# Turned weight blocks routed through device memory, and the value products moved within their step

## The chip, the cores and the metric

The kernel runs on one NeuronCore of one Trainium2 chip. The metric is the device time of that core in microseconds (us), from one execution of the whole program; the median of three runs is compared.

## The reference

Two parts follow one another. The first is an attention with a threshold, for 8 batches of 8 heads, 576 positions and head size 64, in float32:

```python
scores = scale * np.matmul(q, k.transpose(0, 1, 3, 2))          # scale = 1/8
thresh = np.max(scores, axis=-1, keepdims=True) - tau           # tau = 0.02
scores = np.where(scores >= thresh, scores, -1000000000.0)
attn = np.exp(scores - np.max(scores, axis=-1, keepdims=True))
attn = attn / (np.sum(attn, axis=-1, keepdims=True) + 1e-09)
x = np.matmul(attn, v)                                          # heads joined: 4608 tokens x 512
```

The second is an MLP over the 4608 tokens: `h = x @ w_in` (512 to 2048), `g = max(h, 0)**2`, `out = g @ w_out` (2048 to 512).

## The kernel before

**Visits and steps.** The program works on pairs of heads; there are 32 of them (4 per batch). The pairs of the first batch are visited twice, the others once, which makes 36 "visits". A visit has one step for each block of 128 queries (blocks 0 to 3) and one for the last 64 queries (block 4). From visit 12 on, two visits run together ("paired"): the even one begins with block 4 for both, then come blocks 0 to 3 of the even visit and blocks 0 to 3 of the odd one, nine steps in all. There are twelve such double visits, and `late_step` is the loop body for them. The steps before them are built by the body at the end of the file.

**What a step does.** TensorE makes scores into PSUM (`scores_of_two`, L282: on even blocks it makes this step's scores and the next one's). VectorE takes the row maxima (L303), ScalarE the exponents (L318), VectorE compares with the threshold and sums (L330), GpSimd divides (L340). The product with the values needs the weights with the keys on the partitions, so they have to be turned. From visit 11 on this is done in two moves. VectorE transposes 32 x 32 squares into the tile `turned` (`turn_blocks`, L417 to L427). Then DMAs carry squares from one group of 32 partitions to another, into the tile `wT` (`place_blocks`, L437 for blocks 0 to 3, L442 and L450 for block 4). `turned` has two halves of 2304 float32 per partition, used in turn. One half holds a pair of blocks: pair 0 is blocks 0 and 1, pair 1 is blocks 2 and 3, pair 2 is block 4. A block pair 0 or 1 goes over in 16 DMAs: for each of the 4 groups of source partitions (`qb`) and each of the 4 groups of target partitions (`j`) one DMA of 32 partitions x 2304 bytes. All of them are issued on SyncE's queue (SP), which works in order.

**The value product.** `mix` (L486) is 40 matmuls of TensorE that multiply the values by `wT`: the group "one" in PSUM bank 0 reads the columns ONE and LEFT (or ODD and ONE) of `wT`, the group "two" in bank 4 reads the columns TWO, which pair 1 fills. Group one is issued first. `put` copies the result to the tile `xT` on ScalarE (L469, L473, L480). Bank 0 and bank 4 overlap the score areas of even steps. `mixes` says in which step a visit's product stands: for an even visit that is the step of block 3 of the odd visit, for an odd visit the step of block 1 of the next double visit; both are odd steps in which no scores are made. At the last step, END, nothing else is left of the attention.

**What fills the rest.** The MLP is cut into pieces of 8 or 16 matmuls (`piece`, L534, L642, L713, L748), which wait in the deque `waiting`; a chunk of 256 tokens adds its pieces when the value product that completes its tokens has been issued (`add_chunk`). `rate(s)` plans how many us of pieces a step takes, from PIECE_US (1.76), from `other(s)` (what scores and value products take in a step; VALUES_US is 4.8) and from a reserve of three pieces that is to be left when a new chunk comes. `fill(quarter)` issues pieces for a quarter of that. The order of the instructions on each engine is the order in which the program writes them; `after()` and `some_later()` write pending work that follows pieces or prepares them on the other engines.

**In `late_step`** the order was: scores, maxima, exponents, then `values()` (the `mix` of this step if there is one), a quarter of pieces, threshold and divide, a second quarter when the step has no `mix`, `turn_last` (which turns the step before's block and places what `place_at` lists), then the other quarters. `place_at` lists, for a double visit that begins at step s: block 4 at s+1 and s+2, pair 0 and 1 of the even visit at s+3 and s+5, pair 0 and 1 of the odd visit at s+8 and s+9. Their products stand at s+8 and s+11.

Of the kernel before, what the change touches and what calls it, by code (L numbers as in the profile page):

```python
# [9 lines left out]
FP32 = mybir.dt.float32  # L10
# [9 lines left out]
def kernel(  # L20
# [10 lines left out]
    nc = tc.nc  # L31
# [3 lines left out]
    P = 128  # L35
    HP = H // 2
    NPAIR = B * HP
    NBLK = S // P
    REST = S - NBLK * P
# [10 lines left out]
    ctx.enter_context(tc.manual_schedule(engines={getattr(mybir.EngineType, e) for e in MANUAL}))  # L50

    const = ctx.enter_context(tc.tile_pool(name="const", bufs=1))
    psum = ctx.enter_context(tc.tile_pool(name="psum", bufs=1, space=bass.MemoryType.PSUM))

    ident = const.tile([P, P], FP32, name="ident")
# [19 lines left out]
    ODD, ONE, LEFT, TWO = 0, REST, REST + 2 * P, 2 * REST + 2 * P  # L75
    wT = const.tile([P, S // REST + 1, NC9, REST], FP32, name="wT")
# [3 lines left out]
    at = RAW * 2 * WP  # L80
# [12 lines left out]
    NB = 2 * KB * 2 * 32  # L93
    turned = const.tile([P, 2 * NB], FP32, name="turned")
    assert 3 * 3 * WP <= 2 * NB
    g = const.tile([P, NFT, TCH], FP32, name="g")
    gsum = [const.tile([P, HF, P], FP32, name=f"gsum{i}") for i in range(2)]
    held = const.tile([P, 2 * HD], FP32, name="held")
# [97 lines left out]
    def some_loads():  # L196
        for _ in range(min(1 + (len(loads) > 8), len(loads))):
            to, src = loads.popleft()
            (nc.gpsimd if state["step"] > first_dma + 2 else nc.sync).dma_start(out=to, in_=src)
# [193 lines left out]
            nc.scalar.copy(wT[:, 2 * NBLK, NBLK, :], ps[:, 0, 0:D])  # L393

    blocks = {}

    def turn_blocks(vis, i):

        w = weights[vis, i][0]
        two = i < NBLK
        M = KB - 2
        if not two or i % 2 == 0:
            at = len(blocks) % 2 * NB
            t = turned[:, at:at + NB]
            blocks[vis, i // 2] = t.rearrange("p (j c u q) -> p c j u q", j=4, u=2, q=32) if two else t.rearrange("p (k q) -> p k q", q=32)
        wb = blocks[vis, i // 2]  # L410
        move = nc.vector.transpose
        if two:
            wb = wb[:, :, :, i % 2, :]
            whole_, rest_ = (w[:, :, x0 * 32:x1 * 32].rearrange("p u (c j q) -> p u c j q", q=32, j=n)
                             for x0, x1, n in ((0, M, 4), (M, KB, 2)))
            h = M // 4
            move(wb[:, 0:h, :, :], whole_[:, 0, :, :, :])  # L417
            if i < 2:
                move(wb[:, h, :, :].rearrange("p (u j) q -> p u j q", u=2), rest_[:, :, 0, :, :])
            else:  # L420
                move(wb[:, h, 2:4, :], rest_[:, 0, 0, :, :])
                move(wb[:, h, 0:2, :], rest_[:, 1, 0, :, :])
            move(wb[:, h + 1:, :, :], whole_[:, 1, :, :, :])
            return
        parts = [(0, 0, KB, 0), (1, M, KB, KB), (1, 0, M, KB + 2)] if paired(vis) else [(0, 0, KB, 2), (0, M, KB, 0)]
        for u, k0, k1, at in parts:
            move(wb[:, at:at + k1 - k0, :], w[:, u, k0 * 32:k1 * 32].rearrange("p (k q) -> p k q", q=32))  # L427

    def place_blocks(vis, pair, which=range(4)):

        wb = blocks[vis, pair]
        for qb in which:
            rows = slice(qb * 32, qb * 32 + 32)
            for j in range(4):
                to = wT[j * 32:j * 32 + 32, :, :, :]
                if pair < NBLK // 2:
                    nc.sync.dma_start(out=to[:, (ONE, TWO)[pair] // REST + qb, :, :].rearrange("p c q -> p (c q)"),  # L437
                                      in_=wb[rows, :, j, :, :].rearrange("p c u q -> p (c u q)"))
                    continue
                at = slice(qb % 2 * 32, qb % 2 * 32 + 32)  # L440
                if paired(vis):
                    nc.sync.dma_start(out=to[:, (LEFT if qb < 2 else ODD) // REST, :, at], in_=wb[rows, j:2 * KB:4, :])  # L442
                else:


                    first = j if qb < 2 else KB + (j - KB) % 4
                    n = len(range(first, KB if qb < 2 else 2 * KB, 4))
                    c = first // 4
                    first += 2 if qb < 2 else -KB
                    nc.sync.dma_start(out=to[:, LEFT // REST, c:c + n, at], in_=wb[rows, first:first + 4 * n - 3:4, :])  # L450
# [151 lines left out]
    def some_later(engine):  # L602
        if later[engine]:
            make(*later[engine].popleft())
# [201 lines left out]
    steps = [(n, i) for n in range(len(visits)) for i in visits[n][1]]  # L806
    NST = len(steps)

    def by_dma(n):

        return n >= 3 * HP - 1
# [5 lines left out]
    mixes = {}  # L817
# [14 lines left out]
    END = max(mixes)  # L832

    chunk_at, j = {}, 0
# [5 lines left out]
    VALUES_US = 4.8  # L840
    SCORES_US = 1.25
    RESERVE = 3 * PIECE_US
    waiting = deque()
    state = {"us": 0.0, "left": 0.0, "step": 0, "free": False, "rounded": 0, "usable": 0, "then": [], "last": []}

    def early():
        return state["step"] < min(chunk_at)
# [20 lines left out]
    def rate(s):  # L868


        if s < out_from:
            return PIECE_US * sum(x[2] == 0 for x in waiting) / (out_from - s)
        have = PIECE_US * len(waiting) - state["left"]
        best = 1e9
        at = s
        for e in sorted(chunk_at) + [END]:
            if e > s:
                have += sum(other(x) for x in range(at, e))
                at = e
                best = min(best, (have - (RESERVE if e < END else 0)) / (e - s))  # L880
                have += PIECE_US * sum(len(pieces_of(x)) for x in chunk_at.get(e, ()))
        return max(best, 0.0) - other(s)

    def other(s):

        us = VALUES_US if s in mixes and by_dma(mixes[s][0]) else 0.0
        if s < NST:
            n, i = steps[s]
            us += SCORES_US * (1 if s < first_late or i == NBLK else 0 if i % 2 else 2)
        return us  # L890

    def after():
        now = state["last"]
        state["last"] = []
        for fn in state["then"]:
            state["last"] += fn() or []
        state["then"] = []
        for fn in now:
            fn()

    def piece():
        _, fn, *what = waiting.popleft()
        state["left"] -= PIECE_US
        if fn is mlp_out or what[0] <= PLAIN and what[1] == 0:
            after()
        then = fn(*what)
        after()
        state["then"] = then
        if state["step"] >= NST:
            some_later("vector")  # L910
            some_later("gpsimd")

    def fill(us):
        state["left"] += us
        while waiting and state["left"] >= PIECE_US / 2 and waiting[0][0] <= state["usable"]:
            piece()
        state["left"] = min(state["left"], PIECE_US)
# [72 lines left out]
    def turn_last(s):  # L990
        if s <= NST:
            turn_blocks(*steps[s - 1])
        for what in place_at[s]:
            place_blocks(*what)

    def late_step(s):

        on = s < NST
        odd = on and steps[s][1] % 2 == 1
        if on:  # L1000
            n, i = steps[s]
            if not odd:
                scores_of_two(s)
            maxima(s, [area(u, odd) for u in range(2)])
            after()
            some_later("gpsimd")
            exponents(n, i)
        def values():
            if s in mixes:
                while (visits[mixes[s][0]][0] // HP + 1) * S - RING > read_to["x"]:  # L1010
                    piece()
                mix(*mixes[s])
                for j in chunk_at.get(s, ()):
                    add_chunk(j)

        values()
        quarter = rate(s) / 4 if s < END else 1e9
        fill(quarter)
        some_later("vector")
        some_later("gpsimd")  # L1020
        smooth = s not in mixes
        if smooth:
            after()
        if on:
            threshold(n, i)
            for fn in prep_at[s] + load_at[s]:
                fn()
            divide(n, i)
        if smooth:
            fill(quarter)  # L1030
            after()
            some_later("gpsimd")
        turn_last(s)
        some_loads()
        some_later("vector")
        if not smooth:
            some_later("gpsimd")
            fill(quarter)
        some_loads()
        fill(quarter)  # L1040
        some_loads()
        fill(quarter)
        some_loads()

    for s in range(END + 1):
        state["step"] = s
# [83 lines left out]
        if 0 < s <= NST and by_dma(steps[s - 1][0]):  # L1130
            m, x = steps[s - 1]
            turn_blocks(m, x)
        for what in place_at[s]:
            place_blocks(*what)
        some_loads()
# [53 lines left out]
```

## Time and profile before

| | |
|---|---|
| median of 3 runs | 1396.67 us (1395.84 to 1403.11) |
| span of the profiled execution | 1397.5 us, mean granted TensorE clock 0.983 |
| instructions | 25994 |
| L437, DMAs of block pairs 0 and 1 | 800, issue 589 ns each at the median, 507 at the least |
| L442, DMAs of block 4, paired visits | 192, issue 612 ns each |
| L450, DMAs of block 4, visit 11 | 16, issue 602 ns each |
| L486, matmuls of the value products | 1700, 183.7 us of TensorE in all |
| TensorE busy in 330 to 1242 us (attention and MLP together) | 867.5 of 912 us |
| TensorE busy in 1242 to 1398 us (MLP alone) | 151.7 of 156 us |

"Busy" is the time in which an engine works on an instruction. TensorE is named PE in the profile, VectorE DVE, ScalarE ACT, GpSimd POOL; SPq is SyncE's queue, which issues DMAs. The wait views give, for each line, the idle time of an engine before it and what ended that idle time. Where a wait is for several semaphores, the engine named is the one that the profile saw last, and it need not be the right one.

### The profile page before, as it was taken

How to read it: one execution, taken by the hardware profiler on the slowest of the kernel's cores; microseconds unless marked ns; L12 is line 12 of the kernel's file. 1: busy time of each engine (PE TensorE's matmuls, PEld its weight loads, DVE VectorE, ACT ScalarE, POOL GpSimd, SP SyncE). 2: the span in 40 equal slices, each digit the busy share in tenths (PEclk: the TensorE clock that was granted, in tenths of full speed). 3: DMA queues.
4: the chain of work that ended last, by engine and by line, in shares of the span. 5: the costliest groups of instructions: out<-in, count | busy, mean ns of one | idle time of the engine just before them, and what ended most of it. 6: DMA issues, size and time to landing. Idle time of an engine off the chain costs nothing.

```text
span 1397.5 us, 25994 instructions
## 1 busy us (share of the span) xinstructions
PE 1316.7 (94%) x9112; PEld 1086.3 (78%) x9112; DVE 946.3 (68%) x2026; ACT 585.0 (42%) x1357; POOL 975.6 (70%) x1229
## 2 busy tenths in 40 slices
PE   6899999889898989999999989999989999999998
PEld 5676567768686969788887868878778787889997
DVE  6877775867676877767877786758677767732231
ACT  4777673225152534334433434433425252513322
POOL 3789774867786968595978777768585867643451
PEclk8999999989999999999999999999999999999999
DMA  8754431434344444433534443434443334330000
GB/s 154 160 148 142 120 82 30 102 70 98 81 118 104 116 99 107 103 91 87 113 90 107 104 106 84 108 81 103 87 111 86 86 92 91 82 78 1 16 16 16
DMA packets 201555, 128.16 MB, mean 92 GB/s; under 512 B 159664, under 2 KB 164048, under 8 KB 201424
## 3 DMA queue, kind: packets, MB, share of 16 engines
q1 hardware_dynamic: 180832, 95.10, 29.5%
q0 software_dynamic: 18288, 31.11, 8.6%
q8 instruction: 72, 1.18, 0.3%
q10 hardware_dynamic: 2304, 0.29, 0.2%
q14 instruction: 59, 0.48, 0.1%
HBM read 50.59 MB, written 9.44 MB: 43 GB/s over the span
## 4 chain that ended last, share of the span: by engine, by line
PE 77%; DVE 8%; ACT 4%; POOL 4%; issue 3%; SPq 3%; DMA 1%; ACTq 0%; DVEq 0%; POOLq 0%
PE big L748 25%; PE big L642 25%; PE big L486 10%; PE big L282 8%; PE big L534 3%; PE big L266 3%; DVE w L330 3%; DVE st L303 2%; PE big L713 2%; PE big L379 2%; ACT w L318 2%; SPq L437 1%; ACT wT L380 1%; DMA wT<-turned 1%; DVE gsum L772 1%
## 5 line engine op out<-in xcount | busy, mean ns | idle before, releaser
L303 DVE TENSOR_REDUCE st<-big 128x1 f32<-128x576 f32 x288 | 204.0, 747 | 149.1 <-PE big L282 114.9
L330 DVE SCALAR_TENSOR_TENSOR w<-big,st,w 128x576 f32<-128x576 f32 x269 | 208.9, 813 | 93.6 <-ACT w L318 93.4
L748 PE MATMUL big<-wo,gsum 128*128 128x256 f32 x1088 | 245.3, 382 | 1.1 <-DVE gsum L772 1.1
L340 POOL TENSOR_SCALAR w<-w,st 128x576 f32<-128x576 f32 x269 | 227.6, 856 | 22.7 <-DVE st L333 15.0
L748 PEld LDWEIGHTS big<-wo,gsum 128*128 128x128 f32 x1088 | 204.8, 190 | 38.8 <-issue 12.0
L486 PE MATMUL big<-wT,vs 128*64 128x128 f32 (+7 forms) x1700 | 183.7, 375 | 45.3 <-DVE w L330 15.1
L486 PEld LDWEIGHTS big<-wT,vs 128*64 128x64 f32 (+1 forms) x1700 | 102.6, 142 | 120.6 <-issue 32.3
L642 PE MATMUL big<-xT,w_in_sb 128*128 128x128 f32 x1536 | 187.2, 276 | 0.6 <-DVE g L654 0.6
L748 PE MATMUL big<-wo,g 128*128 128x256 f32 x816 | 186.2, 382 | 0.6 <-ACT g L650 0.6
L642 PEld LDWEIGHTS big<-xT,w_in_sb 128*128 128x128 f32 x1536 | 179.4, 192 | 8.0 <-issue 5.4
L318 ACT ACTIVATE w<-big,st 128x576 f32<-128x576 f32 x269 | 183.9, 735 | 0.2 <-ACT st L316 0.2
L338 POOL TENSOR_SCALAR st<-st 128x2 f32<-128x2 f32 (+1 forms) x148 | 35.3, 239 | 205.3 <-DVE w L330 197.6
L748 PEld LDWEIGHTS big<-wo,g 128*128 128x128 f32 x816 | 151.4, 190 | 27.4 <-issue 7.9
L315 ACT ACTIVATE st<-st 128x2 f32<-128x2 f32 (+1 forms) x148 | 30.5, 206 | 270.8 <-DVE st L303 269.7
L654 DVE TENSOR_TENSOR g<-big,g 128x512 f32<-128x512 f32 x96 | 64.8, 676 | 76.6 <-PE big L642 72.0
L282 PE MATMUL big<-kT,qT 64*128 64x256 f32 (+3 forms) x768 | 106.8, 416 | 0.2
L282 PEld LDWEIGHTS big<-kT,qT 64*128 64x128 f32 x768 | 84.4, 186 | 14.5 <-issue 4.3
L524 POOL TENSOR_TENSOR gsum<-g 128x512 f32<-128x512 f32 x34 | 45.3, 1332 | 63.0 <-ACT g L651 62.7
L650 ACT ACTIVATE g<-g 128x512 f32<-128x512 f32 x96 | 60.6, 631 | 63.1 <-DVE g L654 62.9
L651 ACT ACTIVATE g<-g 128x512 f32<-128x512 f32 x128 | 80.9, 632 | 4.1
L417 DVE STREAM_TRANSPOSE turned<-w 128x512 f32<-128x512 f32 x100 | 68.8, 688 | 7.3 <-DMA wT<-turned 6.6
L642 PE MATMUL big<-xT,gsum 128*128 128x128 f32 x512 | 63.7, 277 | 5.1 <-POOL gsum L573 4.7
(119 smaller groups left out, 2261.5 us busy)
## 6 DMA issues: line engine op xcount, KB each, us to landing
wT<-turned SPq DMA_DIRECT2D x800, 72.0 KB, 2.1
wo<-in_moe_w_in_dram SPq DMA_DIRECT2D x16, 512.0 KB, 4.4
wo<-in_moe_w_out_dram SPq DMA_DIRECT2D x16, 512.0 KB, 3.7
out_dram<-osb POOLq DMA_DIRECT2D x32, 256.0 KB, 2.7
ql<-in_q_dram POOLq DMA_DIRECT2D x96, 72.0 KB, 3.0
wT<-turned SPq DMA_DIRECT2D x192, 36.0 KB, 2.1
kl<-in_k_dram POOLq DMA_DIRECT2D x88, 72.0 KB, 3.3
vs<-in_v_dram POOLq DMA_DIRECT2D x48, 128.0 KB, 3.3
```

What stands on the lines that cost most here:

```text
L282: nc.tensor.matmul(big[to, at + x0:at + x1], lhsT, keys[u * D:(u + 1) * D, x0:x1], start=True, stop=True)
L303: nc.vector.tensor_reduce(out=mx[:, u:u + 1], in_=sc[u], axis=AX.XY, op=ALU.max)
L318: nc.scalar.activation(out=w[:, u, :].rearrange("p (h k) -> p h k", h=2), in_=sc[u], func=AF.Exp, bias=bias[:, u:u + 1], scale=SCALE)
L330: nc.vector.scalar_tensor_tensor(out=wu, in0=sc[u], scalar=thr[:, u:u + 1], in1=wu, op0=ALU.is_ge, op1=ALU.mult, accum_out=sm[:, u:u + 1])
L340: nc.gpsimd.tensor_scalar(out=w[:, u, :], in0=w[:, u, :], scalar1=z[:, u:u + 1], scalar2=rcp[:, u:u + 1], op0=ALU.add, op1=ALU.mult)
L417: move(wb[:, 0:h, :, :], whole_[:, 0, :, :, :])
L486: nc.tensor.matmul(ps[u * D:(u + 1) * D, :], vs[n % 2][rows, u * (NBLK + 1) + c, :], wT[rows, at // REST:(at + ps.shape[1]) // REST, NBLK ...
L642: nc.tensor.matmul(to[:, f, :], factor(j, p, q, c)[:, f * P:(f + 1) * P], part[:, c, :], start=(p in "125" and f == 0 and c == 0), stop=(p ...
L650: nc.scalar.activation(out=to, in_=to if src is None else src, func=AF.Relu)
L651: nc.scalar.activation(out=to, in_=to, func=AF.Square)
L654: nc.vector.tensor_tensor(out=x, in0=to, in1=x, op=ALU.add)
L748: nc.tensor.matmul(to, left[:, f, :], wo[:, slot, f, :], start=(f == 0), stop=(f == HF - 1))
```

## The change

The 16 DMAs of a block pair 0 or 1 are replaced by a path through device memory. As soon as the second block of a pair has been turned, `set_aside` writes its whole half of `turned` (128 partitions x 9216 bytes) to one of four areas of a tensor `aside` in device memory, in one DMA. `place_blocks` then reads it back with four DMAs, one for each group of target partitions (32 partitions x 4 runs of 2304 bytes). All five are on SyncE's queue. Block 4 keeps its DMAs.

In `late_step` the value product moves from the start of the step to its middle, after two quarters of pieces, the threshold and the division; all steps now have the same order; END keeps the product at the start. `at_least` makes sure that at least one piece stands ahead of the product within its step, and two behind it. `other` now puts half of a value product on the step before it. The aim is that the copies need fewer issues and that the product comes when its operands are there.

```diff
+    aside = dram.tile([4, P, NB], FP32, name="aside")
...
+    outside = {}
+
+    def set_aside(vis, pair):
+
+        t = aside[len(outside) % 4]
+        at = list(blocks).index((vis, pair)) % 2 * NB
+        nc.sync.dma_start(out=t, in_=turned[:, at:at + NB])
+        outside[vis, pair] = t.rearrange("(b r) (j x) -> r j b x", r=32, j=4)
...
         wb = blocks[vis, pair]
+        if pair < NBLK // 2:
+            for j in range(4):
+                g0 = (ONE, TWO)[pair] // REST
+                nc.sync.dma_start(out=wT[j * 32:j * 32 + 32, g0:g0 + 4, :, :].rearrange("r b c q -> r b (c q)"),
+                                  in_=outside[vis, pair][:, j, :, :])
+            return
         for qb in which:
...
-                if pair < NBLK // 2:
-                    nc.sync.dma_start(out=to[:, (ONE, TWO)[pair] // REST + qb, :, :].rearrange("p c q -> p (c q)"),
-                                      in_=wb[rows, :, j, :, :].rearrange("p c u q -> p (c u q)"))
-                    continue
...
-        us = VALUES_US if s in mixes and by_dma(mixes[s][0]) else 0.0
+        us = sum(VALUES_US / 2 for x in (s, s + 1) if x in mixes and by_dma(mixes[x][0]))
...
             turn_blocks(*steps[s - 1])
+            if steps[s - 1][1] % 2:
+                set_aside(steps[s - 1][0], steps[s - 1][1] // 2)
...
+    def at_least(count, made):
+        while waiting and state["made"] < made + count:
+            piece()
...
-        values()
+        if s == END:
+            values()
         quarter = rate(s) / 4 if s < END else 1e9
+        made = state["made"]
         fill(quarter)
         some_later("vector")
         some_later("gpsimd")
-        smooth = s not in mixes
-        if smooth:
-            after()
+        after()
         if on:
             threshold(n, i)
...
             divide(n, i)
-        if smooth:
-            fill(quarter)
-            after()
-            some_later("gpsimd")
+        fill(quarter)
+        after()
+        some_later("gpsimd")
+        valued = s in mixes and s < END
+        if valued:
+            at_least(1, made)
+            made = state["made"]
+            values()
         turn_last(s)
         some_loads()
         some_later("vector")
-        if not smooth:
-            some_later("gpsimd")
-            fill(quarter)
         some_loads()
         fill(quarter)
         some_loads()
         fill(quarter)
         some_loads()
+        if valued:
+            at_least(2, made)
```

The loop body before `late_step` calls `set_aside` in the same way, for visit 11; `piece` counts the pieces in `state["made"]`.

More of the change, by code (lines that the diff above doesn't have):

```diff
@@ L52 @@
     const = ctx.enter_context(tc.tile_pool(name="const", bufs=1))
+    dram = ctx.enter_context(tc.tile_pool(name="dram", bufs=1, space=bass.MemoryType.DRAM))
     psum = ctx.enter_context(tc.tile_pool(name="psum", bufs=1, space=bass.MemoryType.PSUM))
@@ L843 @@
     waiting = deque()
-    state = {"us": 0.0, "left": 0.0, "step": 0, "free": False, "rounded": 0, "usable": 0, "then": [], "last": []}
+    state = {"us": 0.0, "left": 0.0, "step": 0, "free": False, "rounded": 0, "usable": 0, "then": [], "last": [], "made": 0}
     def early():
@@ L903, in piece @@
         state["left"] -= PIECE_US
+        state["made"] += 1
         if fn is mlp_out or what[0] <= PLAIN and what[1] == 0:
@@ L1132 @@
             turn_blocks(m, x)
+            if x % 2:
+                set_aside(m, x // 2)
         for what in place_at[s]:
```

## Prediction

> **What bounds the kernel now.** I read the page's busy line and its chain first, then TensorE's waits in the stretch where attention and MLP run together, then the timeline around one value product.
>
> ```profile
> PE 1316.7 (94%) x9112; PEld 1086.3 (78%) x9112; DVE 946.3 (68%) x2026; ACT 585.0 (42%) x1357; POOL 975.6 (70%) x1229
> ...
> PE 77%; DVE 8%; ACT 4%; POOL 4%; issue 3%; SPq 3%; DMA 1%; ACTq 0%; DVEq 0%; POOLq 0%
> ```
>
> TensorE is the bound: busy 94%, and 77% of the chain. No part of the change touches the number of its matmuls. So it can gain only TensorE's idle time: 80.8 us in all, of which 44.5 lie in 330 to 1242 us. Who owns those? The waits of PE there (total us, times, longest):
>
> ```profile
> PE big L486 <- DVE w L330: 15.1, 5, 3.8
> PE big L486 <- DVE st L333: 8.0, 2, 4.7
> PE big L642 <- POOL gsum L573: 4.7, 2, 3.3
> PE big L486 <- DVE st L332: 3.6, 1, 3.6
> ...
> PE big L486 <- DMA wT<-turned: 2.7, 1, 2.7
> ```
>
> Nearly all are at L486, the value product, and the view blames the threshold on VectorE. I don't believe that name: the product stands in odd steps, whose scores lie outside bank 0 and bank 4. The timelines of PE and of SP around one such wait, and the landing time under L437, show another owner:
>
> ```profile
> 590.18 2.37 PE L486 MATMUL big<-wT,vs 128*64 128x320 f32 x16
> 596.40 4.27 PE L486 MATMUL big<-wT,vs 128*64 128x256 f32 x24 [3.84 <-DVE w L330]
> ...
> 582.85 10.25 SPq L437 DMA_DIRECT2D wT<-turned  x16
> ...
> DMA to landing us min/median/max: 1.9/2.1/4.5
> ```
>
> Group one runs at 590.18 without a wait. Group two, the only one that reads the columns TWO, stops at 592.56 and goes on at 596.40. Its columns come from sixteen L437 issues that end at 593.10; by the semaphore events of the trace the last landed at 595.96, so 0.44 us before the restart. The same holds for the other odd visits: in ten of twelve double visits the product stops between the groups, for 4.69, 3.56, 3.46, 3.84, 2.39, 2.69, 3.37, 3.29, 0.59 and 1.78 us, together **29.7 us**, each time until just after the last landing of pair 1. The two others landed in time (674.61 for a need at 674.9; at END 1242.99 for 1243.3). The product of even visits, whose pair 1 has three steps of slack, waits once (2.1 us at 803). Visit 11 has its own stall before that stretch: 4.66 and 3.16 us at 275 to 284, for L450's DMAs, which start at 272.03 only because SP was issuing sixteen L437s until 271.93 (their squares had been turned by 266.9).
>
> So the target is 29.7 + 7.8 = 37.5 us of pure DMA wait on the bounding engine.
>
> [...] here 72 KB cost 2.1 us, no less than 256 KB[...] I take it that SP stands still for the whole landing of the write.
>
> **The change part by part.**
>
> 1. *Removed: sixteen issues per pair.* A pair took 10.0 us of issue (582.85 to 593.10), then 1.5 to 3 us to land. From first issue to last landing I read 11.5 to 14.2 us, typically 12.6.
>
> 2. *Added: one write of 1.18 MB.* Each of 16 DMA engines moves 73.7 KB. The trace's packet records have 159 ns for 4096 B (weight loads): 18 x 159 = 2.9 us. The fixed part from the 256 KB store: 2.1 us less its eight 2 KB packets per engine at 86 ns (0.7) = 1.4. Sum **4.3 us**. Upper bound: packets at 220 ns (the median of GpSimd-queue loads of that size)[...]. Taken: 4.5[...].
>
> 3. *Added: four reads of 295 KB each, after a wait.* Issue 0.37 (weight load) to 0.59 (L437) each. A 512 KB load takes 4.1 us at the median, eight 4 KB packets of it 1.3 to 1.8, so some 2.6 fixed. Moving 4 x 8 packets of 2304 B takes 32 x 90 to 125 ns = 2.9 to 4.0. Sum 2.6 + 2.9 = **5.5**, at most 6.9.
>
>    The trip is then **10 us**, between 9.5 and 14.3, against 12.6: nearer by 2.6, or in the worst case later by 1.7. What is queued behind SP's new wait: the four reads, then block 4's DMAs of the next double visit, for which VectorE and TensorE wait one to nine steps later; all q, k and v loads of this stretch go through GpSimd's queue. SP's issue time falls from 800 x 0.59 = 472 us to 50 x 0.4 + 200 x 0.5 = 120, plus 50 waits of 4.5 = 225, so the queue is not fuller than before.
>
> 4. *`turned` is free after the write lands.* 4.5 instead of 12.6 us. VectorE waited 6.6 us for it in 17 places; it is idle a quarter of the stretch, so I cost this at nothing.
>
> 5. *The value product in mid-step.* A double visit is some 79 us (950 us for twelve), 8.8 per step. Before, TensorE came to the product at the step's start. Now the step before has 2.4 us fewer pieces (half of VALUES_US moves there), and (8.8 - 2.4)/2 = 3.2 us of pieces stand ahead in the step. Net, the product comes **0.8 us later** relative to the turning of pair 1. In the five steps in which an odd product completes a batch before END, `rate` doesn't yet see the new chunk, and about one piece (1.76) stands ahead: 0.6 us earlier instead.
>
>    The need: from pair 1's first issue to the end of group one I read 8.4 to 11.9 us, mean 10.4 (582.85 to 592.56 is 9.7). With the shift, 9.8 to 11.2. A trip of 10 us meets this on average; where need is shortest some 1 to 1.5 us are left. I leave 4 us of the 29.7: **25.7 gained**.
>
> 6. *Visit 11.* The wait for SP shortens: write at 261.2 lands by 265.7, four reads are issued by 267.7, so L450 starts at 267.7 instead of 272.0. Of 7.8 us some **4 gained**.
>
> 7. *New waits of TensorE.* The next even step's scores overwrite banks 0 and 4 and need `put`. Two pieces (3.5 us) stand between; `put` takes 1.0 us of ScalarE (0.37, 0.22 and 0.39 at 571) that begins some 0.1 us after the product. Hidden, except where ScalarE comes late. Pieces may run short where a chunk is added half a step later, but the reserve is three pieces, just the one ahead and the two behind. I put **2 us** against the gain.
>
> 8. *`after()` and `some_later` in all steps, `at_least`, the ring of four areas*: order only; VectorE and GpSimd have a quarter of the time free, and an area comes round after four pairs (some 60 us). Nothing. DMA engines: L437's 25600 packets of 155 ns were 248 us of each engine; the new path takes 50 x (2.9 + 2.9 to 4.0) = 290 to 345. The share goes from 38% to 42 to 45%. Nothing waits on that.
>
> Sum: 25.7 + 4 - 2 = 27.7; 1396.7 - 27.7 = **1369 us**.
>
> **The rivals.**
>
> *The round trip costs as much as the sixteen issues.* For it: [...] the read cannot begin before the write is down. Against: the 2.1 us of the 256 KB store. At 14.3 us against a need of 10.9, 3.4 us of each of eleven stalls remain; the gain is 4 from the other terms, about **1390**.
>
> *Slower: the product in mid-step stops TensorE in a new way.* ScalarE's `put` and the bank reuse would stand in front of the next scores, in all 23 products, and the chunk's pieces come later by half a step. If each product lost 2 us, and the five batch ends 3 more, that is 61; less 33 of DMA waits gone: **1424**; at half of it, 1394. I take **1404** for the case. For it: step chains of 6.6 us (maxima 1.4, exponents 1.9, threshold 1.6, division 1.7) leave only 2 us of slack in 8.8. Against: the two pieces behind the product.
>
> *All of it and more.* Both stall groups and half of the 10 us at L642 go: 1397 - 37.5 - 5 = **1354 to 1358**. For it: GpSimd's work is spread more evenly. Against: those waits have other causes (L573).
>
> **How the numbers follow.** Forecast 0.62 (1362 to 1378), more 0.07, small gain 0.15 (half of it inside 0.5%), slower 0.16 (a little of it inside 0.5%). Faster by over 0.5% is below 1389.7: 0.62 + 0.07 + 0.08 = 0.77. Same 0.09, slower 0.14. The range goes from the upper gain, 1358, to just above the small gain, 1394; what is left out is most of the slower case and a little below.
>
> **What would show it.** In the profile after: fifty issues aside<-turned of 1152 KB landing in 4 to 5 us and two hundred wT<-aside of 288 KB, in place of 800; a DMA trip near 10 us from the write's issue to the last read's landing. PE's waits at L486 in 330 to 1242 us fall from some 32 to under 8 us, TensorE busy time stays at 1317 within 1%. The span after the last product stays at 152 us. I am wrong if L486 keeps its waits (the trip is too long), or if they go and L282 or L642 wait instead (bank reuse, lack of pieces). L450 should begin near 268 us.

## The result, and the profile after

The changed kernel takes **1419.28 us** (median of four runs, 1415.47 to 1422.79) against 1399.54 for the kernel before in the same comparison: a ratio of 1.0141 (95% interval 1.0095 to 1.0187). Run again beside the experiments it gave 1.0123 (1.0102 to 1.0143). The forecast was 1369. So the change is slower by 1.2 to 1.4%.

The page of the kernel after: busy line, chain, and the first two lines of its DMA issues (KB each, median us from issue to landing).

```profile
PE 1321.9 (93%) x9112; PEld 1090.5 (77%) x9112; DVE 944.6 (67%) x2026; ACT 584.0 (41%) x1357; POOL 977.7 (69%) x1229
...
PE 72%; DVE 8%; POOL 6%; DMA 5%; ACT 4%; issue 3%; SPq 1%; ACTq 0%; DVEq 0%; POOLq 0%
...
aside<-turned SPq DMA_DIRECT2D x50, 1152.0 KB, 4.7
wT<-aside SPq DMA_DIRECT2D x200, 288.0 KB, 5.4
```

The number of matmuls is the same, and TensorE is still the bound. On the chain DMA went from 1% to 5%: the round trip is now part of what ends last. The waits of PE in 330 to 1242 us of the kernel after (total us, times, longest; the value product is now L498, scores L284, the MLP lines L654 and L760):

```profile
PE big L498 <- DMA wT<-aside: 13.5, 4, 4.1
PE big L498 <- DVE st L335: 7.7, 3, 3.4
PE big L654 <- ACT g L674: 6.9, 1, 6.9
PE big L654 <- POOL gsum L585: 4.9, 3, 2.3
PE big L498 <- DVE turned L433: 4.2, 1, 4.2
...
PE big L760 <- DVE gsum L780: 3.3, 1, 3.3
PE big L284 <- DVE qT L242: 3.0, 2, 2.1
```

The waits that were to go are still there: 29 us at L498, with two lines left out here. Beside them stand new ones, before MLP pieces (L654, L760) and before scores (L284). The same product as the one shown of before, in the timelines of PE and SP:

```profile
599.82 2.38 PE L498 MATMUL big<-wT,vs 128*64 128x320 f32 x16
606.27 4.94 PE L498 MATMUL big<-wT,vs 128*64 128x256 f32 x24 [4.08 <-DMA wT<-aside]
```

```profile
592.12 0.34 SPq L404 DMA_DIRECT2D aside<-turned  x1
598.38 1.73 SPq L445 DMA_DIRECT2D wT<-aside  x4
601.54 14.91 SPq L454 DMA_DIRECT2D wT<-turned  x16
```

The write is issued at 592.12 and lands 6.2 us later (the slowest of the fifty; the median is 4.7). Only then does SP issue the first read, at 598.38, and by the trace's semaphore events the last read lands at 606.13. That is a trip of 14.0 us. Group one ended at 602.20, so TensorE stood still for 4.08 us, somewhat longer than the 3.84 of before.

One more thing is lost there. In the kernel before, the 24 matmuls behind the wait took 4.27 us, while in a product without a wait all 40 took 4.79. The windows view of the kernel before (us, then busy us of each engine, then PEclk, the granted TensorE clock) for the wait at 592.56 and the stretches behind it:

```profile
593.00:596.40 3.40, 0.00 (x0) 0.03 (x1) 1.67 (x4) 1.66 (x4) 3.38 (x5) 1.00 0.73 142
596.70:600.10 3.40, 3.40 (x20) 2.01 (x20) 1.70 (x5) 0.00 (x0) 3.22 (x6) 0.50 0.31 48
600.10:603.50 3.40, 3.40 (x21) 2.58 (x15) 0.84 (x2) 0.76 (x3) 3.30 (x6) 1.00 0.22 35
```

TensorE idles through the first stretch, runs at **half clock** (0.50) for the next 3.4 us, and is back at 1.00 after that. Such a wait is paid for partly twice (here 3.84 us of standing still, then 3.41 us at half clock), and the prediction priced it once. Which waits are followed by half clock is taken up in the last section.

For the whole execution I add up two things from the trace: gaps of TensorE of more than 0.1 us (without the one ahead of its first matmul), and half-clock time after 240 us. Before: 73.5 and 34.1 us. After: 86.3 and 47.8 us. The gaps account for 12.8 us of the 17.5 us between the two profiled spans; TensorE's busy time rose by 5.2 us with the same matmuls, which fits the 13.7 us more of half clock.

### The profile page after: what moved, and what is told of

Read it like the earlier page. It is cut to its first block, busy times and chain, and to the rows that moved or that the text cites. A ratio compares the mean times of both kernels' runs of the same rounds, so it can differ in the third digit from the quotient of the medians.

```text
span 1415.0 us, 25269 instructions
## 1 busy us (share of the span) xinstructions
PE 1321.9 (93%) x9112; PEld 1090.5 (77%) x9112; DVE 944.6 (67%) x2026; ACT 584.0 (41%) x1357; POOL 977.7 (69%) x1229
## 3 DMA queue, kind: packets, MB, share of 16 engines
q8 instruction: 72, 1.18, 0.4%
q10 hardware_dynamic: 2304, 0.29, 0.2%
## 4 chain that ended last, share of the span: by engine, by line
PE 72%; DVE 8%; POOL 6%; DMA 5%; ACT 4%; issue 3%; SPq 1%; ACTq 0%; DVEq 0%; POOLq 0%
PE big L654 23%; PE big L760 22%; PE big L498 9%; PE big L284 7%; PE big L546 3%; PE big L268 3%; DVE st L305 2%; DMA wT<-aside 2%; DVE w L332 2%; DMA aside<-turned 2%; PE big L725 2%; PE big L381 2%; ACT w L320 2%; POOL g L585 1%; POOL vs L201 1%
## 5 line engine op out<-in xcount | busy, mean ns | idle before, releaser
L342 POOL TENSOR_SCALAR w<-w,st 128x576 f32<-128x576 f32 x269 | 232.9, 875 | 23.4 <-DVE st L335 16.5
L760 PE MATMUL big<-wo,gsum 128*128 128x256 f32 x1088 | 246.0, 383 | 3.3 <-DVE gsum L780 3.3
L760 PEld LDWEIGHTS big<-wo,gsum 128*128 128x128 f32 x1088 | 205.3, 191 | 42.2 <-issue 8.9
L498 PE MATMUL big<-wT,vs 128*64 128x128 f32 (+7 forms) x1700 | 181.1, 372 | 41.6 <-DMA wT<-aside 15.0
L498 PEld LDWEIGHTS big<-wT,vs 128*64 128x64 f32 (+1 forms) x1700 | 100.8, 141 | 116.8 <-issue 35.3
L654 PE MATMUL big<-xT,w_in_sb 128*128 128x128 f32 x1536 | 187.8, 277 | 2.3 <-DVE g L666 1.9
L654 PEld LDWEIGHTS big<-xT,w_in_sb 128*128 128x128 f32 x1536 | 180.5, 193 | 7.8 <-issue 3.7
L760 PE MATMUL big<-wo,g 128*128 128x256 f32 x816 | 186.4, 382 | 0.0
L760 PEld LDWEIGHTS big<-wo,g 128*128 128x128 f32 x816 | 151.2, 190 | 26.1 <-issue 7.5
L317 ACT ACTIVATE st<-st 128x2 f32<-128x2 f32 (+1 forms) x148 | 30.3, 205 | 303.0 <-DVE st L305 302.0
L284 PE MATMUL big<-kT,qT 64*128 64x256 f32 (+3 forms) x768 | 108.5, 421 | 5.1 <-DVE qT L242 5.1
L284 PEld LDWEIGHTS big<-kT,qT 64*128 64x128 f32 x768 | 86.0, 189 | 20.6 <-DVE qT L242 6.3
L654 PE MATMUL big<-t,g 128*128 128x128 f32 x512 | 65.0, 285 | 11.6 <-ACT g L674 6.9
L654 PEld LDWEIGHTS big<-t,g 128*128 128x128 f32 x512 | 61.4, 198 | 15.8 <-ACT g L674 7.1
```

What stands on the lines that cost most here:

```text
L284: nc.tensor.matmul(big[to, at + x0:at + x1], lhsT, keys[u * D:(u + 1) * D, x0:x1], start=True, stop=True)
L342: nc.gpsimd.tensor_scalar(out=w[:, u, :], in0=w[:, u, :], scalar1=z[:, u:u + 1], scalar2=rcp[:, u:u + 1], op0=ALU.add, op1=ALU.mult)
L498: nc.tensor.matmul(ps[u * D:(u + 1) * D, :], vs[n % 2][rows, u * (NBLK + 1) + c, :], wT[rows, at // REST:(at + ps.shape[1]) // REST, NBLK ...
L654: nc.tensor.matmul(to[:, f, :], factor(j, p, q, c)[:, f * P:(f + 1) * P], part[:, c, :], start=(p in "125" and f == 0 and c == 0), stop=(p ...
L760: nc.tensor.matmul(to, left[:, f, :], wo[:, slot, f, :], start=(f == 0), stop=(f == HF - 1))
```

## The experiments

All ratios are to the kernel before on the same chip, with 95% intervals. "Gaps" and "half clock" are the two sums just named, in us, from each kernel's profile. e0 to e3 ran on one chip, e4 to e7 on a second, e8 to e10 on a third, e11 and e12 on one each; between these groups only the ratios are compared.

| run | ratio (interval) | gaps | half clock |
|---|---|---|---|
| kernel before | 1 | 73.5 | 34.1 |
| e0: the change again | 1.0123 (1.0102 to 1.0143) | 82.6 | 51.2 |
| e1: device memory only | 1.0062 (1.0044 to 1.0081) | 78.1 | 47.8 |
| e2: order and planning only | 1.0109 (1.0091 to 1.0127) | 81.7 | 54.6 |
| e3: pair 1 on two queues | 1.0342 (1.0318 to 1.0366) | 99.4 | 88.8 |
| e4: before, pieces between groups | 0.9839 (0.9816 to 0.9861) | 52.5 | 20.5 |
| e5: e1, pieces between | 0.9850 (0.9825 to 0.9875) | 53.1 | 30.7 |
| e6: e2, pieces between | 0.9979 (0.9965 to 0.9993) | 64.1 | 44.4 |
| e7: e2, old planning | 1.0178 (1.0154 to 1.0201) | 90.5 | 61.4 |
| e8: e6, batch ends at the start | 0.9915 (0.9896 to 0.9935) | 58.2 | 23.9 |
| e9: e4, also visit 11 | 0.9847 (0.9825 to 0.9869) | 50.4 | 10.2 |
| e10: e1, reads in order 0, 2, 1, 3 | 1.0054 (1.0036 to 1.0072) | 75.0 | 47.8 |
| e11: e8, planned where it stands | 0.9909 (0.9888 to 0.9929) | 56.6 | 27.3 |
| e12: e4, new sequence of posts | 0.9900 (0.9877 to 0.9923) | 55.4 | 27.3 |

### The change taken apart: e0, e1, e2

Theory A: the device memory path does the harm. Theory B: the new order does. e1 has the path with `late_step` and `other` of before; e2 has the new order, planning and `at_least` with the sixteen DMAs.

> The changed kernel itself, beside the others on one chip, so that its parts can be compared with the whole. Both theories: 1.010 to 1.019 of before. If it is inside 0.5% of before here, the slowdown is a matter of the chip and not of the change.

> Device memory path alone, order and planning of before. Theory A (the path is the harm: its trip is 13.4 us where the plan had 10, against 12.6 before, and its traffic makes the other loads land later): all of the slowdown or more, 1.012 to 1.025, with the waits of the value product between its groups 0.5 to 1 us longer than before each. Theory B (the order is the harm: the product in mid-step holds up scores and copies): 1.000 to 1.006.

> Product in mid-step, halves of its planned time and the least numbers of pieces, with the sixteen DMAs of before. Theory A: not slower than before, 0.980 to 0.997, since the product comes about 0.6 us later relative to its blocks and a trip of 12.6 us then misses the need of 11.0 by 1.6 us instead of about 3. Theory B: 1.010 to 1.020, with new idle time of TensorE before scores and before the MLP pieces.

Neither theory holds alone. The path costs 0.6%, the order 1.1%, both together 1.2%, so they are not additive. How each misses its aim can be measured at eleven products of odd visits (the twelfth, at END, is not moved by the change). Take the time from the end of the turning of pair 1 (VectorE) to two events, the end of group one (the need) and the last landing of the blocks; the table gives the means, and the sum of the waits between the groups:

| | need | landing | waits, eleven products |
|---|---|---|---|
| before | 10.4 us | 12.7 us | 29.7 us |
| e1, device memory | 10.4 us | 13.7 us | 38.5 us |
| e2, order | 11.0 us | 12.8 us | 25.6 us |
| e0, both | 11.0 us | 13.6 us | 30.1 us |

Device memory makes the blocks land 1.0 us later, not earlier. The order makes the need come 0.6 us later, where 2.3 would have been wanted. With both, the later need takes back most of what the later landing costs at these products, which is part of why the two costs don't add up. In e2 the waits at the product stay (longest 4.7 us), and new ones stand beside them. PE's waits of e2 in 330 to 1242 us:

```profile
PE big L486 <- DMA wT<-turned: 12.4, 4, 4.7
PE big L486 <- DVE st L333: 9.6, 3, 3.5
PE big L642 <- ACT g L662: 5.3, 1, 5.3
PE big L642 <- POOL g L573: 4.8, 5, 1.4
PE big L748 <- DVE gsum L768: 3.3, 1, 3.3
PE big L282 <- DVE qT L240: 3.0, 2, 2.1
```

The last four lines hold most of what the order adds: TensorE waits for ScalarE, GpSimd and VectorE to prepare its MLP pieces and its scores. In this stretch the waits at L642 are 17.1 us in e2 and 10.8 before, those at L748 3.3 and 1.7, those at L282 3.0 and none.

### Is the landing what stops the product? e3

```diff
-                    nc.sync.dma_start(out=to[:, (ONE, TWO)[pair] // REST + qb, :, :]...
+                    queue = nc.scalar if pair == 1 and paired(vis) and vis % 2 and j % 2 else nc.sync
+                    queue.dma_start(out=to[:, (ONE, TWO)[pair] // REST + qb, :, :]...
```

> Kernel and order of before; of the sixteen DMAs of pair 1 of the odd visits, the eight of two target groups are issued on ScalarE's queue beside the other eight on SyncE's, so the last lands some 4.5 us earlier; no traffic is added. If the late landing is what stops the product in before (my reading of its profile), the waits between its groups fall from 29.7 us to under 3 and the time to 0.970 to 0.982. If the threshold named by the wait view were the owner, or if TensorE had no use for the time, 0.995 to 1.010.

The first half of the expectation came out: no product of the paired stage waits between its groups any more. That alone doesn't settle the owner, because in e3 two things changed: over the same eleven products the blocks land 9.3 us after the turning instead of 12.7, but group one also ends 18.7 us after it instead of 10.4, which would have hidden a late threshold too. The restarts of group two settle it. In the kernel before, all ten waits end 0.41 to 0.44 us after the last landing, while the last threshold instruction on VectorE ended anywhere from 0.02 to 5.6 us ahead of them. In e1, which has the order of before and later landings, all eleven end 0.13 to 0.20 us after the last landing. So the landing is the owner, and the threshold that the wait view names is not.

The time of e3 went the other way, by 3.4%. The timelines of PE and then of ACT in e3, just ahead of a product:

```profile
592.64 2.21 PE L282 MATMUL big<-kT,qT 64*128 64x256 f32 x14
600.40 1.22 PE L282 MATMUL big<-kT,qT 64*128 64x256 f32 x2 [5.56 <-ACT seen L295]
```

```profile
592.79 7.36 ACTq L438 DMA_DIRECT2D wT<-turned  x8
600.19 0.16 ACT L295 COPY seen<-big 128x1 f32<-128x1 f32 x1 [11.35 <-DMA wT<-turned]
```

Eight issues hold ScalarE's queue for 7.4 us. Behind them in that queue waits the small copy `seen` (L295), which the last two score matmuls need. TensorE stops for 5.56 us there, eleven such stops take 56.3 us, and the half clock of the whole run rose to 88.8 us. A wait of 30 us was traded for one of 56, because of what stood behind the issues in that queue.

### Filling the wait instead: e4, e5, e6

In `mix`, between the groups:

```diff
         for ps, x, _ in groups:
+            if x == TWO and paired(n) and n % 2:
+                for _ in range(min(2, len(waiting))):
+                    piece()
             for c in range(NBLK):
```

> Kernel and order of before; in the product of an odd visit of the paired stage two MLP pieces (some 3.5 us) are issued between group one and group two, so TensorE has work while the last blocks land. Theory A (the wait between the groups and the half clock that follows it are lost time of the bounding engine): waits between the groups fall from 29.7 to under 8 us, the half-clock spells of the paired stage from some 27 us to under 10, time 0.970 to 0.982 of before. Theory C (the step's chain of scores, maxima, exponents and turning sets the pace, and the time is given back elsewhere): 0.993 to 1.003, with new idle time before scores or pieces.

> Device memory path with the order of before, and two pieces between the groups. Landing is 13.7 us after turning and need then about 14.2. If the path harms only through the later landing: within 0.005 of the run with sixteen DMAs and pieces between. If its traffic harms by itself (later loads, stores): 0.008 or more above that run.

> The change's order and planning with sixteen DMAs, and two pieces between the groups. If the order harms only because the product still meets blocks that have not landed: within 0.005 of the run with the order of before and pieces between. If the order has a cost of its own (idle time before scores and before MLP pieces that wait for ScalarE copies): 0.008 to 0.015 above that run.

e4 is 1.6% **faster than before**: the theory of lost TensorE time holds, though the gain is just short of its range (0.970 to 0.982). The half clock of the paired stage fell from 23.9 to 10.2 us. A product in the timeline of PE in e4:

```profile
744.13 2.37 PE L486 MATMUL big<-wT,vs 128*64 128x320 f32 x16
746.43 2.05 PE L645 MATMUL big<-xT,w_in_sb 128*128 128x128 f32 x16
748.32 1.95 PE L645 MATMUL big<-xT,gsum 128*128 128x128 f32 x16
750.20 2.63 PE L486 MATMUL big<-wT,vs 128*64 128x256 f32 x24
```

The same blocks land as late as ever (12.8 us after the turning against a need of 10.4), but group two starts at 750.20 without a gap: its 24 matmuls take 2.63 us, not 4.27. The waits at L486 after 330 us fell to 1.4 us. Some of the gain was given back: the waits at L642 (here L645) grew from 11.2 to 16.7 us, those before scores from 0.1 to 3.8.

e5 differs from e4 by 0.0011, inside both intervals. So with the wait filled, the device memory path costs nothing that can be measured, although the loads of `kl` land in 5.4 us instead of 3.3 in the changed kernel's page. Within these intervals its traffic does no harm here; what it costs in e1 is its later landing.

e6 is 1.4% above e4. The order therefore has a cost of its own. Its largest single wait, in PE's timeline of e6, comes after a product that completes a batch:

```profile
602.31 3.84 PE L645 MATMUL big<-xT,w_in_sb 128*128 128x128 f32 x32
617.40 2.93 PE L645 MATMUL big<-t,g 128*128 128x128 f32 x12 [11.25 <-POOL t L622]
```

TensorE waits 11.25 us for GpSimd to make the token differences of the new chunk. In the changed kernel the longest new wait (6.9 us, the L654 line above) stands behind the same batch end and ends with ScalarE.

### What of the order costs: e7, e8, e11, e12

e7 is e2 with `other` of before. e8 moves the products that complete a batch (five of the paired stage, and visit 11's) back to the start of their step:

```diff
-        if s == END:
+        at_start = s == END or s in chunk_at
+        if at_start:
             values()
...
-        valued = s in mixes and s < END
+        valued = s in mixes and not at_start
```

e11 also plans those products wholly in their own step. e12 has all products at the start and planned there, so that of the order only one thing is left beside e4: in product steps `after()`, a quarter of pieces and `some_later` stand ahead of `turn_last`, as in the other steps.

> The change's order with sixteen DMAs, but the planned time of a product counted wholly in its own step, as before. If the halving makes the new idle time before scores (L282, 5.1 us) and pieces: 1.000 to 1.005, and that idle time is gone. If the place of the product makes it: 1.008 to 1.014 as with the halving.

> The change's order with sixteen DMAs and two pieces between the groups, except that the five products that complete a batch (and add a chunk of tokens) stand at the start of their step, as before; the others stay in mid-step. If the order's own cost of 18 us comes from chunks that are added half a step later (TensorE waiting at L645 for GpSimd's token differences, 11.25 us at 606): those waits fall from 25.0 us to near 17 and the time to 0.984 to 0.990 of before. If it comes from the place of every product or from the planning: 0.994 to 1.000.

> As the run with batch ends at the start of their step, but the planned time of those products is counted wholly in their own step, as before; only mid-step products are halved. In that run the waits of the value product rose from 15.9 to 30.3 us. If the rise comes from the halving (2.4 us fewer pieces ahead of a product that stands at the start, so that it meets its blocks earlier): those waits return to 15 to 20 us with the waits at L645 staying near 10, time 0.980 to 0.986 of before. If it comes from something else in the mixed order: 0.989 to 0.993 as there.

> Sixteen DMAs, pieces between the groups, all products at the start of their step and planned there, as in the run with pieces between (0.9839); what is left of the change is that steps with a product now write their pending posts and their second quarter of pieces ahead of the turning, like the other steps. If that sequence makes the 0.7% that remains when batch ends are moved back (0.9909): 0.989 to 0.993. If the six other products in mid-step make it: 0.981 to 0.986.

e7 lies above both of its ranges: the halving is no cause of the slowdown. Without it the order costs 1.8% instead of 1.1%, and the gaps before scores rise from 5.1 to 13.3 us.

e8: the waits at L645 fell from 25.0 to 10.3 us, lower than expected, and the one of 11.25 us shrank to 1.65. But the time came down only by half, since the waits at the product rose from 15.9 to 30.3 us: at batch ends the need was 6.6 to 8.1 us after the turning there, 9.7 to 12.0 in e4. e11 shows that this rise came from the halving, since all waits of value products are 16.1 us there; but the time stayed (0.9909), and the waits at L645 came back to 21.7 us (the long one stayed away, at 1.79). Waits of nearly the same sum had only changed places. So a chunk that is added half a step later made the 11.25 us wait; that it made the other waits at L645 isn't shown.

e12 gives 0.9900 where e4 gave 0.9839; the intervals just miss each other. So the new sequence of posts alone costs some 0.6%, about what is left in e11. The rest of e6's 1.4%, 0.6 to 0.7%, went with the batch ends, in e8 and e11 alike. That the other products in mid-step cost nothing (six of odd visits, and the twelve of even visits, which the expectation of e12 leaves out) follows only by subtraction, at the limit of these intervals. Which post in the new sequence does the harm isn't settled: in e12 the gaps are 2.9 us above e4, nearly all of it before scores (L282, 6.8 us against 3.8), and the half clock is 6.8 us above.

### Two smaller questions: e9, e10

e9 adds four pieces ahead of visit 11's product and two between its groups. e10 issues e1's four reads for target groups 0, 2, 1, 3.

> Kernel and order of before with two pieces between the groups in the paired stage, and in the product of visit 11 four pieces (7 us) ahead of group one and two between, to fill the wait of 8 us and the half clock of 10.2 us there. If a filled wait pays here too: 6 to 12 us less than the run with two pieces alone, 0.975 to 0.980 of before. If visit 11's time is given back (the pieces are then missing in the first double visit): within 0.002 of 0.984.

> Device memory path with the order of before; the four reads are issued for target groups 0, 2, 1, 3 instead of 0, 1, 2, 3. Each read writes 32 partitions, and its packets of 2304 B took 180 ns at the median where the shortest took 93. If neighbours in the queue overlap [...]: packets fall to 130 ns or less, a read-back from 7.9 to under 6.8 us, time some 3 to 8 us below the run without it (1.0062). [...]

e9 gave nothing that can be measured beyond e4: the gaps at the product fell from 15.1 to 8.2 us, those at the MLP line rose from 16.7 to 21.9, of which 5.8 stand in the first double visit. The pieces were missing there, as the second expectation said.

e10 fell well short of the gain in its expectation (130 ns, 6.8 us). The 2304 B packets took 161 ns instead of 179, the read-back 7.5 us instead of 7.8, and the ratio can't be told from e1's. What this order of the reads changes is a small part of the slow read at most.

## Why the prediction was wrong

**What held.** TensorE is the bound. The owner of the waits at L486 is the landing of pair 1 and not the named threshold (e3, e4). The write: 4.7 us measured, 4.5 taken. SP frees visit 11's DMAs earlier: L450's successors begin at 267.69 us, forecast 267.7; the gaps there fell from 7.8 to 5.35 us, 2.5 gained where 4 was forecast. The span behind the last product stayed at 151 us. And recovering the wait does pay: e4 gains 22 us, near the 25.7 us of part 5, by another edit.

**Part 3 failed: the read.** It was taken as 5.5 us, at most 6.9; it took 7.9 at the median of 50. The working used 90 to 125 ns for a packet of 2304 B, the quick end of what the trace of before had for that size; its median there was 155 ns, and I used that number myself in part 8. In the changed kernel it was 180. With it the same sum gives 2.6 us + 32 x 180 ns = 8.4, with 155 ns 7.6; and the 5.5 was the low end of the range that the sum had (2.6 plus 2.9 to 4.0). The landing of one read in the kernel after shows it too (us from issue, under L445):

```profile
DMA to landing us min/median/max: 3.4/5.4/9.4
```

Why the packets of the read take so long is not shown. They moved 2304 B in 180 ns at the median (12.8 B/ns), those of the write 9216 B in 355 ns (26 B/ns). No run here varies the read in anything but the order of the four, and e10 shows that this order is not the way around it (161 ns).

So the trip was 13.4 us at the median (12.3 for sixteen issues, read as 12.6 in part 1), not 10. The waits that it was to remove stayed. The DMA engines' share rose from 38.7 to 53.5% on the pages, where part 8 had 42 to 45. This is the first rival, "the round trip costs as much as the sixteen issues", and it would have given 1390 only if the rest had gone as forecast. The 14.3 us that it took for the trip, the upper end in part 3, was my estimate, which the trace of before doesn't show; the longest trip measured was 14.9. Two small slips change nothing: the issue time in part 1 is 10.25 us by its own times, not 10.0, and the upper terms of part 3 add up to 6.6, not 6.9.

**Part 5 fell with part 3.** The shift was put at 0.8 us, and at minus 0.6 at batch ends. Measured in e0 against before, it is 0.8 on average over the six products that end no batch, but between minus 1.5 and 3.5 for single ones, so the agreement is partly luck; at the five batch ends it is 0.4 later, not earlier. The need in the changed kernel is 10.1 to 13.7 us after the turning. A trip of 10 us would have met all eleven to within 0.2 us (an estimate from these figures); the real one met one. So of the 25.7 us that part 5 counted on nothing was gained.

**Parts 7 and 8 failed: the new waits.** They were priced at 2 us and at nothing. The working looked at `put`, the banks and the number of pieces in reserve, but not at the other engines' preparation of the pieces. The runs show that preparation (11.25 us on GpSimd at one batch end of e6), and 0.6% for the posts in another sequence, which part 8 had called order only (e12): together 1.4% in e6 against e4. e6 also suggests that a quicker trip alone would not have saved the forecast: with the waits between the groups filled, the order still leaves 0.9979 of before, where 1369 us is 0.980. The second rival had the batch ends in it, at 3 us each, and its range up to 1424 holds the result. Its other reason, `put` and the banks in front of the next scores, does not show: the waits before scores are 5.1 us in the kernel after, all for `qT` from VectorE.

**A price that was missing.** A wait was costed at its own length. The traces show half clock behind most waits of over 3 us (before: behind seven of nine after 240 us). In e3 gaps rose by 26 us and busy time by 23; the span grew by 48.5.

## What to carry to other kernels

Before moving a transfer to make it land earlier, measure two times from the moment its source is ready, the landing and the need, and price the new path with the median packet of the same size (here 155 ns before and 180 after, where 90 to 125 were taken). Where an engine stops for a transfer, as TensorE did here for up to 4.69 us, work of the same engine that doesn't depend on it, issued between the part that is ready and the part that isn't, can be worth more than a quicker transfer: here two pieces gave 1.6% on the kernel before, 2.1% on the device memory path and 1.3% on the new order. When an issue or a product is moved, look at the queue of the engine that gets it, for the small instruction behind it that the bound engine waits for (in e3 the copy `seen`, 56.3 us in eleven stops).

## What the hardware showed that I had not expected

The half clock didn't follow every wait by its length alone. In the kernel before, a wait of 2.39 us at 750 was followed by 3.4 us of it, one of 4.69 us at 361 by 6.8 us, and waits of 3.56 us at 441 and 2.69 us at 835 by none. The trace has a pattern. In it, all changes of the granted clock after 240 us lie on a fixed grid of 3.41 us (half clock begins at 279.22, 364.56, 518.16, 596.66, 753.68, 917.52 and 999.44, whole multiples of 3.413 us apart), and half clock begins behind those stretches of the grid in which TensorE was least busy. The windows view of before, on that grid:

```profile
439.65:443.07 3.42, 1.65 (x14) 0.59 (x10) 3.42 (x7) 1.67 (x4) 3.42 (x6) 1.00 0.64 158
443.07:446.48 3.41, 1.62 (x16) 1.26 (x16) 3.10 (x9) 0.00 (x0) 3.39 (x5) 1.00 0.69 101
750.27:753.68 3.41, 1.02 (x12) 0.86 (x12) 1.89 (x6) 1.36 (x3) 3.41 (x5) 1.00 0.46 98
753.68:757.09 3.41, 3.41 (x20) 1.45 (x17) 1.50 (x3) 0.33 (x2) 3.39 (x6) 0.50 0.75 137
```

The wait of 3.56 us at 441 lies across two stretches and leaves TensorE busy for 1.65 and 1.62 us of them, nearly half: the clock stays at 1.00. The shorter wait at 750 lies inside one stretch and leaves 1.02 us, 0.30 of it: the next stretch runs at 0.50. In this profile the clock fell after stretches that were busy for at most 0.38, and stayed after all that were busy for at least 0.41. In the kernel after, the changes are whole multiples of 3.413 us apart too, but the clock fell after a stretch that was busy for 0.43 (1.48 of 3.42 us, at 383.39), so no single share divides the stretches of both profiles. Two waits of nearly one length had different costs: the one of 3.46 us at 515 left TensorE busy for 0.38 us of its stretch and was followed by 3.41 us of half clock, the one of 3.56 us at 441 by none.

The issue of one DMA of 128 partitions x 9216 B took SP 0.34 us, less than the 0.59 us for one of 32 partitions x 2304 B between partition groups; 1.18 MB went out in the time of eight of those small issues.
